# Rows of one more unit by DMA transpose, row stores moved behind two loads, and a hand-written end with stores by column halves

## The chip, the cores and the metric

The kernel runs on one core of one Trainium2 chip. The metric is the device time of one execution in microseconds (us); the time before is the median of three runs.

## The reference

Two stages follow each other, for 8 batches, 12 heads, 448 tokens and head dimension 64:

```
scores = q @ k.T / sqrt(64);  attn = max(scores, 0)**2 / 448;  o = attn @ v
x = o with the heads side by side            # (8, 448, 768)
s = x @ w_gate                               # one score per token
top = the 128 tokens of the batch with the highest score
out = x;  out[top] = x[top] + sigmoid(s[top]) * (max(x[top] @ w1, 0) @ w2)
```

`w1` is 768 x 1024, `w2` is 1024 x 768. Inputs and output are float32; the kernel computes in bfloat16 with float32 accumulation.

## The kernel before

The attention is cut into 24 units of four heads; unit u belongs to batch u // 3. Per unit the steps are: `L` loads q, k and v (a casting DMA from POOL's queue), `T` and `TE` transpose q and k on TensorE and copy them out of PSUM, `S` computes scores, `R` applies the relu on ACT or VectorE, `Q` squares, `V` multiplies with v, and `X` copies the result out as `xT_sb`, which holds x transposed: features on partitions, tokens along the row.

The rows of x (tokens on partitions, `x_rows`, tile name x_sb) are made from `xT_sb` in one of two ways. `XR` (lines 265 to 273) does eight TensorE transposes into a PSUM pair and `XE` (line 275) copies them out; `XB` (line 282) does two DMA transposes, issued from SP. Units up to 14 use the first way, units from 15 on the second. `ST` (line 291) stores the rows of a batch to the output from POOL's queue, four DMAs a batch.

The mixture-of-depths part of a batch is the class `Moe`. `g` and `bc` give the scores along the row, `col` gives them down the partitions, `rk`, `cs`, `rank` and `hot` make `hot_`, a 0/1 matrix that picks the 128 tokens by rank. `sel`, `xe` and `xeE` gather the tokens (as `xeT`), `h` and `hE` do the first layer, `gs` and `sig` the gate, `y` and `yE` the second layer times the gate (tile `gye`), and `ADD` adds the result to the stored rows by an indirect DMA from POOL.

The last batch (7) does not go through `ST` and `ADD`. There the rows are put together on TensorE: for each of four chunks c of the tokens, `xa` multiplies the rows by a permuted identity (`ident_2`) into a PSUM pair, and `od` adds the second layer's result by `hotT`, the transposed `hot_` (`ht`, `htE`). The result is split into a high and a low bfloat16 part, `yH` on ACT and `yL` on VectorE. `oE` copies a chunk out of PSUM and `OS` stores it, from SP's queue. Chunk 3 has 64 rows, the others 128. The columns come in two halves of 384, h = 0 and 1; the two halves of a tile lie in the two banks of one PSUM pair. `hq` and `yq` are `h` and `y` in parts.

The order of all instructions is written out by hand in the string `ORDER`; every item is a call, and each engine and queue takes its instructions in that order. Four PSUM pairs (0 to 3) are shared by all steps; the last number of an item that opens a tile in PSUM names its pair, and the item waits until the pair's last user is done. Waits between engines are put in from the tiles that instructions read and write. Line numbers of helpers recur in the profile: L187 is any copy on ACT, L191 a copy on VectorE, L299 any matmul of the `Moe` class, L270 the transposes of `XR`, L288 the DMA transposes of `XB`, L294 the stores of `ST`, L510 the stores of `OS`.

Of the kernel before, what the change touches and what calls it, by code (L numbers as in the profile page):

```python
# [7 lines left out]
FP32 = mybir.dt.float32  # L8
# [12 lines left out]
def kernel(  # L21
# [13 lines left out]
    B, H, S, Dh = q.shape  # L35
    HD = H * Dh
    F = moe_w1.shape[1]
    CAP = int(moe_capacity)
    NC = 7
# [16 lines left out]
    gye_pool = ctx.enter_context(tc.tile_pool(name="gye", bufs=3))  # L56
# [6 lines left out]
          for n in "qkv"}  # L63
# [3 lines left out]
    bc_sb = [const.tile([128, NK * 128], FP32, name=f"bc_sb{i}") for i in range(NX)]  # L67

    stage = {n: const.tile([128, 2, NC * Dh], FP32, name=f"{n}f") for n in "qk"}
    fin = [stage[n].rearrange("p a b -> p (a b)")[:, :HD].rearrange("p (a d) -> p a d", a=2)  # L70
           for n in "qk"]
    wgr = const.tile([NM, 128], FP32, name="wgr")
    wgb = const.tile([NM, 128], BF16, name="wgb")
    unit_f = const.tile([1, 1], FP32, name="unit_f")
# [2 lines left out]
    ident_2 = const.tile([128, 128], BF16, name="ident_2")  # L77
# [93 lines left out]
    def pair(at, shape, dt, name):  # L171
        return ps_pool.tile(shape, dt, name=name, tag=f"pair{at}")
# [12 lines left out]
    def put(eng, out_, in_, func=None, scale=1.0):  # L185
        if eng == "A":
            nc.scalar.activation(out=out_, in_=in_, func=func or AF.Copy, scale=scale)  # L187
        elif func == AF.Relu:
            nc.vector.tensor_scalar(out=out_, in0=in_, scalar1=0.0, scalar2=None, op0=ALU.max)  # L189
        elif isinstance(scale, float) and scale == 1.0:  # L190
            nc.vector.tensor_copy(out=out_, in_=in_)  # L191
        else:
            nc.vector.tensor_scalar(out=out_, in0=in_, scalar1=scale, scalar2=None, op0=ALU.mult)

    t_ps, qkt, s_ps, r_sb, o_ps, xr_ps, x_rows = {}, {}, {}, {}, {}, {}, {}
# [102 lines left out]
    def mm(out_, lhsT, rhs, start, stop, **kw):  # L298
        nc.tensor.matmul(out=out_, lhsT=lhsT, rhs=rhs, start=start, stop=stop,  # L299
                         skip_group_check=True, **kw)  # L300

    class Moe:
# [151 lines left out]

        def yq(self, half, part, at=None):
            if at is not None:
                self.y_ps = [pair(at, [CAP, 2, 512], FP32, "y_ps")] * 2
                self.y_done = [0, 0]
            for f in range(4 * part, 4 * part + 4):
                self.y(half, f)  # L460

# [20 lines left out]
                out=self.yp["L", half], in0=self.y_ps[half][:, half, :384],  # L482
                scalar=self.g_[:, 0:1], in1=self.yp["H", half], op0=ALU.mult, op1=ALU.subtract)

        def xa(self, c, at):
            self.o_ps = getattr(self, "o_ps", {})
            self.o_ps[c] = pair(at, [128, 2, 512], FP32, "od_ps")
            for h in range(2):
                mm(self.o_ps[c][:self.n_out(c), h, :384], self.side(ident_2, c),
                   x_rows[self.b][:, c, 384 * h:384 * h + 384], True, False)  # L490

        def od(self, c, l, h):
            mm(self.o_ps[c][:self.n_out(c), h, :384], self.side(self.hotT[:, c, :], c),
# [7 lines left out]
            return t if c + 4 < NC else t[:, ::2]  # L501

        def oE(self, c, h, eng):
            if c == len(fin):
                fin.append(gye_pool.tile([CAP, 2, 384], FP32, name="gye"))
            n = self.n_out(c)
            put(eng, fin[c][:n, h], self.o_ps[c][:n, h, :384])

        def OS(self, c):
            nc.sync.dma_start(  # L510
                out=out[self.b].rearrange("(p c) d -> p c d", c=NC)[:, c::4],
                in_=fin[c][:self.n_out(c)].rearrange("p a d -> p (a d)"))

        def yE(self, half, eng):
            j = slice(0, 2) if half == 2 else slice(half, half + 1)
# [62 lines left out]
    S,15,2,0 T,16,q,3 V,13,1,0,2 L,k,7,0,2 V,13,2,1 R,15,2,A V,13,3,2 S,15,0,1 V,13,4,3 Q,14,4,7,D L,q,7,0,2  # L578
    V,13,5,4 V,13,6,5 R,15,0,A V,14,1,0,0 V,13,0,6 ADD,2 V,14,2,1 V,14,3,2 X,13,A cs,3,1 TE,16,b,D V,14,4,3
    V,14,5,4 V,14,6,5 V,14,0,6 S,15,3,2 L,v,6,0,2 rank,3 hot,3 X,14,A S,15,1,3 g,4,0,0,4,1 R,15,3,D R,15,1,A  # L580
    XR,14,0 g,4,4,4,6 L,v,6,2,4 XE,14,D sel,3,3 XR,13,2 bc,4,A sE,3,0 Q,15,0,4,D S,15,4,0 XE,13,A xe,3,4 xe,3,5
    xe,3,1 xe,3,3 R,15,4,A xe,3,0 xe,3,2 ST,4,3 col,4 sE,3,1 xeE,3,2,A S,15,5,0 ST,4,1 colE,4 rk,4,0 S,15,6,2
    S,16,4,1 R,15,5,A ST,4,0 h,3,0,3 R,15,6,D h,3,3 ST,4,2 R,16,4,A h,3,7 rk,4,1 S,16,2,0 S,16,0,2 rk,4,2 R,16,2,A
    h,3,2 rk,4,3 h,3,5 Q,15,4,7,D h,3,1 R,16,0,A S,16,1,0 T,17,q,1 T,17,k,1 R,16,1,A S,16,6,2 h,3,4 TE,17,b,D
    L,q,7,2,4 R,16,6,A h,3,6 V,15,1,0,0 L,k,7,2,4 V,15,2,1 hE,3,2,A S,16,5,1 S,16,3,2 V,15,3,2 R,16,5,D V,15,4,3
    V,15,5,4 R,16,3,A V,15,6,5 V,15,0,6 T,18,q,3 Q,16,4,7,D T,18,k,3 X,15,A S,17,0,1 L,v,6,4,6 y,3,0,0,2 y,3,1,0
    y,3,0,1 y,3,1,1 R,17,0,A S,17,6,0 TE,18,b,D XB,15 y,3,0,5 y,3,1,5 R,17,6,A y,3,0,2 y,3,1,2 L,k,7,4,6 S,17,3,1
    Q,16,0,4,D S,17,1,3 R,17,3,A S,17,2,0 L,q,7,4,6 y,3,0,6 y,3,1,6 y,3,0,7 y,3,1,7 R,17,2,A gs,3,1 y,3,0,4
# [21 lines left out]
    rk,6,3 V,21,5,4 Q,22,4,7,D V,22,1,0,1 ADD,5 V,21,6,5 V,21,0,6 R,23,2,A cs,6,2 V,22,2,1 V,22,3,2 X,21,A rank,6  # L610
    S,23,0,0 hot,6 S,23,1,2 ST,6,1 V,22,4,3 V,22,5,4 R,23,0,A R,23,1,D V,22,6,5 ST,6,2 V,22,0,6 XB,21 sel,6,3
    X,22,A ST,6,0 S,23,6,0 sE,6,0 Q,23,0,4,D S,23,4,2 ST,6,3 xe,6,4 R,23,4,A xe,6,5 xe,6,3 xe,6,1 xe,6,0 R,23,6,A
    xe,6,2 g,7,0,0,4,2 sE,6,1 XB,22 xeE,6,2,A Q,23,4,7,D VO,23,0 V,23,1,0,1 V,23,2,1 V,23,3,2 h,6,0,3 h,6,1
    V,23,4,3 V,23,5,4 V,23,6,5 V,23,0,6 h,6,2 X,23,A,0 X,23,D,1 h,6,4 h,6,3 h,6,7 XB,23 h,6,6 h,6,5 colm,7,0,4
    hE,6,2,A colm,7,4,6 g,7,4,4,6 gs,6,0 rk,7,2 y,6,0,0,3 y,6,1,0 sig,6 rk,7,3 y,6,0,3 y,6,1,3 rk,7,1 y,6,0,5
    y,6,1,5 y,6,0,2 y,6,1,2 rk,7,0 y,6,0,4 y,6,1,4 y,6,0,7 y,6,1,7 cs,7,2 y,6,0,1 y,6,1,1 rank,7 hot,7 y,6,0,6
    y,6,1,6 yE,6,2,A Z,p xa,7,0,1
    ht,7,2 xeh,7,0,0 htE,7,D xeh,7,1,2 ADD,6 xeE,7,0,A hq,7,0,0,0 xeE,7,1,A hq,7,0,1 hq,7,1,0,2 hE,7,0,A hq,7,1,1
    gs,7,0 yq,7,0,0,3 hE,7,1,A sig,7 yq,7,1,0 yq,7,1,1 yq,7,0,1 xa,7,1,2 xa,7,2,0 yH,7,1 yH,7,0 yL,7,1 yL,7,0
    od,7,0,H,1 od,7,1,H,1 od,7,2,H,1 od,7,0,H,0 od,7,1,H,0 od,7,2,H,0 od,7,0,L,1 od,7,0,L,0  # L620
    oE,7,0,1,A oE,7,0,0,A od,7,1,L,1 od,7,1,L,0 oE,7,1,1,D oE,7,1,0,D OS,7,0 OS,7,1
    od,7,2,L,1 od,7,2,L,0 oE,7,2,1,A oE,7,2,0,A OS,7,2 xa,7,3,3 od,7,3,H,1 od,7,3,L,1 od,7,3,H,0 od,7,3,L,0
    oE,7,3,1,D oE,7,3,0,A OS,7,3
    """

    ms = {}
# [49 lines left out]
```

## Time and profile before

| | |
|---|---|
| median of three runs | 210.66 us (209.9, 210.66, 211.75) |
| the profiled execution | 210.09 us, of which the span of the profile is 208.3 us |
| TensorE busy | 182.9 us (88% of the span) |
| VectorE busy | 175.1 us (84%) |
| ACT busy | 170.2 us (82%) |
| POOL busy | 111.2 us (53%) |
| chain that ended last | TensorE 59%, ACT 20%, VectorE 8%, POOL 5%, DMA 3%, issue 2% |
| HBM read, written | 39.32 MB, 13.76 MB: 255 GB/s over the span |

Busy time is summed over the instructions of an engine. The chain is followed back from the last instruction of the span, at each step to what released it, so it tells which engine's work could not have been later; an engine can be busy for long and hardly stand in it. Times in rows are us from the start of the span, durations of single instructions ns or us as the column says.

### The profile page before, as it was taken

How to read it: one execution, taken by the hardware profiler on the slowest of the kernel's cores; microseconds unless marked ns; L12 is line 12 of the kernel's file. 1: busy time of each engine (PE TensorE's matmuls, PEld its weight loads, DVE VectorE, ACT ScalarE, POOL GpSimd, SP SyncE). 2: the span in 40 equal slices, each digit the busy share in tenths (PEclk: the TensorE clock that was granted, in tenths of full speed). 3: DMA queues.
4: the chain of work that ended last, by engine and by line, in shares of the span. 5: the costliest groups of instructions: out<-in, count | busy, mean ns of one | idle time of the engine just before them, and what ended most of it. 6: DMA issues, size and time to landing. Idle time of an engine off the chain costs nothing.

```text
span 208.3 us, 8440 instructions
## 1 busy us (share of the span) xinstructions
PE 182.9 (88%) x3781; PEld 119.0 (57%) x3781; DVE 175.1 (84%) x239; ACT 170.2 (82%) x219; POOL 111.2 (53%) x187
## 2 busy tenths in 40 slices
PE   1697866779999999999999999999999899997970
PEld 0443532545676666756855576567557645675730
DVE  3899998999999998998999998997989999742050
ACT  3399998999997989899989699998998989533250
POOL 7987867675677748679393945453243005303000
PEclk9999999999999999999999999999999999999996
DMA  6999999999999999999999998999397040993306
GB/s 190 166 170 201 205 201 204 207 204 202 209 315 338 215 163 168 315 131 168 174 205 260 161 283 158 145 155 134 67 283 119 6 99 5 247 223 41 61 35 229
DMA packets 35967, 36.78 MB, mean 177 GB/s; under 512 B 12566, under 2 KB 32028, under 8 KB 35932
## 3 DMA queue, kind: packets, MB, share of 16 engines
q0 software_dynamic: 25072, 31.60, 83.2%
q1 hardware_dynamic: 10860, 4.66, 12.6%
q8 instruction: 29, 0.48, 0.9%
q14 instruction: 6, 0.05, 0.1%
HBM read 39.32 MB, written 13.76 MB: 255 GB/s over the span
## 4 chain that ended last, share of the span: by engine, by line
PE 59%; ACT 20%; DVE 8%; POOL 5%; DMA 3%; issue 2%; POOLq 0%; ACTq 0%; DVEq 0%
ACT r_sb L187 15%; PE y_ps L299 11%; PE o_ps L250 11%; PE s_ps L228 10%; PE h_ps L299 10%; PE sc_ps L299 4%; PE xe_ps L299 4%; PE t_ps L209 4%; DVE r_sb L240 4%; DMA k_sb<-in_k_dram 3%; ACT xT_sb L187 3%; DVE r_sb L189 2%; PE xr_ps L270 2%; ACT gye L187 2%; PE od_ps L299 1%
## 5 line engine op out<-in xcount | busy, mean ns | idle before, releaser
L187 ACT ACTIVATE r_sb<-s_ps 128x896 bf16<-128x896 f32 x142 | 122.3, 943 | 10.6 <-PE s_ps L228 10.0
L240 DVE TENSOR_TENSOR r_sb<-r_sb 128x3584 bf16<-128x3584 bf16 (+1 forms) x48 | 85.0, 1785 | 2.4 <-ACT r_sb L187 1.4
L228 PE MATMUL s_ps<-qkt 64*64 64x448 bf16 x680 | 57.4, 377 | 6.4 <-ACT r_sb L187 4.3
L250 PE MATMUL o_ps<-r_sb,v_sb 64*64 64x448 bf16 x672 | 42.7, 351 | 2.9 <-issue 1.4
L228 PEld LDWEIGHTS <-qkt 64*64 64x64 bf16 x680 | 21.8, 108 | 24.8 <-issue 17.0
L519 POOL DMA_INDIRECT out_dram<-gye,idx x7 | 13.5, 1922 | 33.7 <-DVE mask L347 15.7
L189 DVE TENSOR_SCALAR r_sb<-s_ps 128x896 bf16<-128x896 f32 x26 | 28.1, 1087 | 2.7 <-PE s_ps L228 2.6
L105 POOL DMA_DIRECT2D v_sb<-in_v_dram x48 | 28.8, 683 | 0.5 <-DMA k_sb<-in_k_dram 0.4
L250 PEld LDWEIGHTS <-v_sb 64*64 64x64 bf16 x672 | 20.3, 106 | 12.3 <-issue 5.6
L191 DVE COPY qkt<-t_ps 128x1792 bf16<-128x1792 bf16 x24 | 25.9, 1084 | 0.8 <-PE t_ps L209 0.7
L299 PE MATMUL y_ps<-w_sb,hT 128*128 128x384 bf16 x128 | 25.5, 327 | 0.0
L299 PE MATMUL h_ps<-xeT,w_sb 128*128 128x128 bf16 x384 | 24.9, 219 | 0.2 <-ACT xeT L187 0.2
L101 POOL DMA_DIRECT2D q_sb<-in_q_dram x23 | 17.4, 754 | 13.9 <-PE t_ps L209 8.5
L299 PEld LDWEIGHTS <-w_sb 128*128 128x128 bf16 x384 | 21.7, 98 | 4.9 <-issue 4.4
L187 ACT ACTIVATE xT_sb<-o_ps 128x896 bf16<-128x896 f32 (+1 forms) x22 | 20.5, 932 | 3.6 <-PE o_ps L250 2.1
L101 POOL DMA_DIRECT2D k_sb<-in_k_dram x23 | 17.1, 744 | 9.1 <-PE s_ps L228 4.4
L294 POOL DMA_DIRECT2D out_dram<-x_sb x28 | 15.6, 625 | 11.5 <-DMA x_sb<-xT_sb 5.5
L103 POOL DMA_DIRECT2D v_sb<-in_v_dram x24 | 17.0, 710 | 7.0 <-PE s_ps L228 3.2
L299 PEld LDWEIGHTS <-hT 128*128 128x128 bf16 x128 | 10.3, 97 | 9.1 <-issue 4.3
L209 PE MATMUL t_ps<-ident,q_sb 64*64 64x64 bf16 x672 | 10.6, 200 | 5.5 <-POOL slot_i L148 4.6
L209 PEld LDWEIGHTS <-q_sb 64*64 64x64 bf16 x672 | 9.5, 113 | 8.2 <-ACT q_sb L187 4.6
L209 PE MATMUL t_ps<-ident,k_sb 64*64 64x64 bf16 x672 | 10.7, 200 | 2.1 <-ACT k_sb L187 1.1
(144 smaller groups left out, 190.5 us busy)
## 6 DMA issues: line engine op xcount, KB each, us to landing
out_dram<-x_sb POOLq DMA_DIRECT2D x21, 384.0 KB, 5.4
q_sb<-in_q_dram POOLq DMA_DIRECT2D x23, 224.0 KB, 6.2
k_sb<-in_k_dram POOLq DMA_DIRECT2D x23, 224.0 KB, 5.9
v_sb<-in_v_dram POOLq DMA_DIRECT2D x24, 112.0 KB, 5.7
v_sb<-in_v_dram POOLq DMA_DIRECT2D x48, 56.0 KB, 5.3
w_sb<-in_moe_w_dram POOLq DMA_DIRECT2D x8, 192.0 KB, 6.4
w_sb<-in_moe_w_dram POOLq DMA_DIRECT2D x6, 256.0 KB, 6.7
out_dram<-x_sb POOLq DMA_DIRECT2D x7, 192.0 KB, 4.8
```

Source lines behind the costliest of these rows:

```text
L101: nc.gpsimd.dma_start(out=t, in_=s_)
L103: nc.gpsimd.dma_start(out=t[:, 0], in_=s_[:, 0])
L105: nc.gpsimd.dma_start(out=t[64 * h:64 * h + 64, 1], in_=s_[64 - 64 * h:128 - 64 * h, 1])
L187: nc.scalar.activation(out=out_, in_=in_, func=func or AF.Copy, scale=scale)
L189: nc.vector.tensor_scalar(out=out_, in0=in_, scalar1=0.0, scalar2=None, op0=ALU.max)
L191: nc.vector.tensor_copy(out=out_, in_=in_)
L209: nc.tensor.matmul(out=t_ps[u][64 * w:64 * w + 64, g, o:o + 64], lhsT=s_[rows, w, c * Dh:c * Dh + Dh], rhs=ident[rows, rows], is_transpose ...
L228: nc.tensor.matmul(out=s_ps[u, c][64 * (g ^ w):64 * (g ^ w) + 64, w, :S], lhsT=qkt[u][rows, g, S + c * 64:S + c * 64 + 64], rhs=qkt[u][row ...
L240: (nc.gpsimd if eng == "P" else nc.vector).tensor_tensor(out=a, in0=a, in1=a, op=ALU.mult)
L250: nc.tensor.matmul(out=o_[64 * g:64 * g + 64, w, :S], lhsT=sb["v"][u % NR][rows, w, c * Dh:c * Dh + Dh], rhs=r_sb[u][rows, c, w, :], start ...
L294: nc.gpsimd.dma_start(out=out[b].rearrange("(p c) d -> p c d", c=NC)[:, 4 * g + k0:4 * g + k0 + n], in_=x_rows[b][64 * g:64 * g + 64, k0:k ...
L299: nc.tensor.matmul(out=out_, lhsT=lhsT, rhs=rhs, start=start, stop=stop, skip_group_check=True, **kw)
```

## The change

Three parts of the order change, with the helpers that they call.

- `XR,14` and `XE,14` are replaced by `XB,14`, two DMA transposes from SP at the place where `XR,14` stood.
- The four `ST,4` items, which stood spread over the items after `xeE,3` and `colE,4`, now stand together behind `L,q,7,2,4 L,k,7,2,4`.
- The end of batch 7 is written anew. `Z,p`, which makes `ident_2` on ACT, moves from behind `yE,6` to before the last square. `xa` takes a column half; `yq` gives each column half its own PSUM pair; `oE` has a tile for each chunk and half; `OS` stores one column half, or both for chunk 2. Both halves of chunk 2 share a new `gye` tile; the halves of chunk 3 use two of the `bc_sb` tiles.

```diff
+    fin = {(c, h): fin[c][:, h:h + 1] for c in range(2) for h in range(2)}
+    for h in range(2):
+        fin[3, h] = bc_sb[h][:, None, :384]
...
         def yq(self, half, part, at=None):
             if at is not None:
-                self.y_ps = [pair(at, [CAP, 2, 512], FP32, "y_ps")] * 2
-                self.y_done = [0, 0]
+                self.y_ps = getattr(self, "y_ps", [None, None])
+                self.y_ps[half] = pair(at, [CAP, 2, 512], FP32, "y_ps")
+                self.y_done = getattr(self, "y_done", [0, 0])
...
-        def xa(self, c, at):
-            self.o_ps = getattr(self, "o_ps", {})
-            self.o_ps[c] = pair(at, [128, 2, 512], FP32, "od_ps")
-            for h in range(2):
-                mm(self.o_ps[c][:self.n_out(c), h, :384], self.side(ident_2, c),
-                   x_rows[self.b][:, c, 384 * h:384 * h + 384], True, False)
+        def xa(self, c, h, at=None):
+            if at is not None:
+                self.o_ps = getattr(self, "o_ps", {})
+                self.o_ps[c] = pair(at, [128, 2, 512], FP32, "od_ps")
+            mm(self.o_ps[c][:self.n_out(c), h, :384], self.side(ident_2, c),
+               x_rows[self.b][:, c, 384 * h:384 * h + 384], True, False)
...
         def oE(self, c, h, eng):
-            if c == len(fin):
-                fin.append(gye_pool.tile([CAP, 2, 384], FP32, name="gye"))
             n = self.n_out(c)
-            put(eng, fin[c][:n, h], self.o_ps[c][:n, h, :384])
-
-        def OS(self, c):
+            if (c, h) not in fin:
+                t = gye_pool.tile([CAP, 2, 384], FP32, name="gye")
+                fin.update({(c, 0): t[:, 0:1], (c, 1): t[:, 1:2], (c, 2): t})
+            put(eng, fin[c, h][:n, 0], self.o_ps[c][:n, h, :384])
+
+        def OS(self, c, h):
+            j = slice(0, 2) if h == 2 else slice(h, h + 1)
             nc.sync.dma_start(
-                out=out[self.b].rearrange("(p c) d -> p c d", c=NC)[:, c::4],
-                in_=fin[c][:self.n_out(c)].rearrange("p a d -> p (a d)"))
+                out=out[self.b].rearrange("(p c) (a d) -> p c a d", c=NC, a=2)[:, c::4, j],
+                in_=fin[c, h][:self.n_out(c)])
...
-    XR,14,0 g,4,4,4,6 L,v,6,2,4 XE,14,D sel,3,3 XR,13,2 bc,4,A ...
+    XB,14 g,4,4,4,6 L,v,6,2,4 sel,3,3 XR,13,2 bc,4,A ...
...
-    ... xeE,3,2,A S,15,5,0 ... ST,4,3 col,4 ... ST,4,1 colE,4 ... ST,4,0 h,3,0,3 ... ST,4,2 R,16,4,A ...
+    L,q,7,2,4 R,16,6,A h,3,6 V,15,1,0,0 L,k,7,2,4 V,15,2,1 ST,4,3 ST,4,1 ST,4,0 ST,4,2 hE,3,2,A ...
...
-    y,6,1,6 yE,6,2,A Z,p xa,7,0,1
-    ht,7,2 xeh,7,0,0 htE,7,D xeh,7,1,2 ADD,6 xeE,7,0,A hq,7,0,0,0 xeE,7,1,A hq,7,0,1 hq,7,1,0,2 hE,7,0,A hq,7,1,1
-    gs,7,0 yq,7,0,0,3 hE,7,1,A sig,7 yq,7,1,0 yq,7,1,1 yq,7,0,1 xa,7,1,2 xa,7,2,0 yH,7,1 yH,7,0 yL,7,1 yL,7,0
-    od,7,0,H,1 od,7,1,H,1 od,7,2,H,1 od,7,0,H,0 od,7,1,H,0 od,7,2,H,0 od,7,0,L,1 od,7,0,L,0
-    oE,7,0,1,A oE,7,0,0,A od,7,1,L,1 od,7,1,L,0 oE,7,1,1,D oE,7,1,0,D OS,7,0 OS,7,1
-    od,7,2,L,1 od,7,2,L,0 oE,7,2,1,A oE,7,2,0,A OS,7,2 xa,7,3,3 od,7,3,H,1 od,7,3,L,1 od,7,3,H,0 od,7,3,L,0
-    oE,7,3,1,D oE,7,3,0,A OS,7,3
+    y,6,1,6 yE,6,2,A xa,7,0,0,1
+    xeh,7,0,0 xeh,7,1,2 ADD,6 xeE,7,0,A ht,7,3 htE,7,D xeE,7,1,A hq,7,0,0,0 hq,7,0,1 gs,7,3 hq,7,1,0,2 hE,7,0,A sig,7
+    hq,7,1,1 yq,7,1,0,3 xa,7,0,1 hE,7,1,A yq,7,1,1 yH,7,1 xa,7,1,1,2 yL,7,1 xa,7,1,0 yq,7,0,0,0 yq,7,0,1
+    yH,7,0 od,7,0,H,1 od,7,1,H,1 yL,7,0 od,7,0,L,1 oE,7,0,1,A OS,7,0,1 od,7,1,L,1 oE,7,1,1,A OS,7,1,1
+    xa,7,2,1,3 xa,7,2,0 od,7,2,H,1 od,7,2,L,1 od,7,2,H,0 od,7,0,H,0 od,7,0,L,0 oE,7,0,0,D OS,7,0,0
+    od,7,2,L,0 oE,7,2,1,A od,7,1,H,0 od,7,1,L,0 oE,7,1,0,A OS,7,1,0 oE,7,2,0,D OS,7,2,2
+    xa,7,3,1,0 xa,7,3,0 od,7,3,H,1 od,7,3,L,1 od,7,3,H,0 od,7,3,L,0 oE,7,3,1,D oE,7,3,0,A OS,7,3,1 OS,7,3,0
```

## Rows read from the trace of the kernel before

**Rows 1.** Chain that ended last, last 20 us: start, length, what
```profile
189.56 0.22 ACT ident L187
...
200.04 2.08 PE od_ps L299 x11
```

**Rows 2.** Timeline of the end: start, length, engine, line, operation, count, idle before
```profile
188.05 0.69 DVE L368 TENSOR_TENSOR hot__4649<-slot_row,rank__4652 128x512 bf16<-128x512 bf16 x1
...
189.83 0.50 PE L299 MATMUL od_ps<-x_sb,ident 128*128 128x384 bf16 x2 [1.25 <-ACT ident L187]
...
190.38 1.77 PE L299 MATMUL xe_ps<-hot__4649,x_sb 128*128 128x128 bf16 x24
190.58 0.69 DVE L191 CAST hotT<-ht_ps 128x512 bf16<-128x512 f32 x1 [1.84 <-PE ht_ps L299]
191.25 0.49 ACT L187 ACTIVATE xeT<-xe_ps 128x384 bf16<-128x384 f32 x1 [1.48 <-PE xe_ps L299]
...
192.00 2.91 PE L299 MATMUL h_ps<-xeT,w_sb 128*128 128x128 bf16 x48
...
193.60 0.60 ACT L187 ACTIVATE hT<-h_ps 128x512 bf16<-128x512 f32 x1 [0.92 <-PE h_ps L299]
...
194.90 2.76 PE L299 MATMUL y_ps<-w_sb,hT 128*128 128x384 bf16 x16
...
197.49 0.81 PE L299 MATMUL od_ps<-x_sb,ident 128*128 128x384 bf16 x4
197.75 1.05 ACT L187 ACTIVATE yH<-y_ps,g__4655 128x384 bf16<-128x384 f32 x2 [2.15 <-PE y_ps L299]
...
198.84 1.14 DVE L481 SCALAR_TENSOR_TENSOR yL<-y_ps,g__4655,yH 128x384 bf16<-128x384 f32 x2 [7.56 <-ACT yH L187]
...
202.73 0.48 ACT L187 ACTIVATE gye<-od_ps 64x384 f32<-64x384 f32 x1 [0.69 <-DVE gye L191]
```

**Rows 3.** Timeline of SP's DMA issues, last 11 us
```profile
201.29 0.66 SPq L510 DMA_DIRECT2D out_dram<-qf  x1
202.05 0.54 SPq L510 DMA_DIRECT2D out_dram<-kf  x1
202.68 1.41 SPq L510 DMA_DIRECT2D out_dram<-gye  x2
```

**Rows 4.** DMA issues of the end: count, KB each, us from issue to landing
```profile
out_dram<-qf SPq DMA_DIRECT2D x1, 384.0 KB, 2.8
...
out_dram<-gye SPq DMA_DIRECT2D x1, 192.0 KB, 3.6
```

**Rows 5.** Windows: length, busy PE, PEld, DVE, ACT, POOL, PEclk, DMA share, GB/s
```profile
3.00:3.50 0.50, 0.00 (x0) 0.00 (x0) 0.00 (x0) 0.00 (x0) 0.50 (x1) 1.00 1.02 384
...
188.00:188.50 0.50, 0.50 (x4) 0.12 (x2) 0.47 (x2) 0.00 (x0) 0.00 (x0) 1.00 0.08 10
...
202.50:202.70 0.20, 0.00 (x0) 0.00 (x0) 0.19 (x1) 0.00 (x0) 0.00 (x0) 1.00 0.51 200
...
203.00:203.50 0.50, 0.00 (x0) 0.00 (x0) 0.00 (x0) 0.21 (x1) 0.00 (x0) 1.00 1.00 399
```

**Rows 6.** Timeline of SP: the last two DMA transposes
```profile
184.10 3.24 SPq L288 DMA_TRANSPOSE x_sb<-xT_sb  x2
```

**Rows 7.** Chain that ended last, 117 to 155 us
```profile
117.94 0.45 PE xr_ps L270 x8
...
138.05 1.45 PE xe_ps L299 x24
...
153.52 0.48 PE t_ps L209 x56
```

**Rows 8.** Timeline of VectorE and POOL, 118 to 130 us
```profile
118.43 0.69 DVE L191 COPY x_sb<-xr_ps 128x1024 bf16<-128x1024 bf16 x1 [0.39 <-PE xr_ps L270]
...
121.65 1.57 POOL L294 DMA_DIRECT2D out_dram<-x_sb  x3 [0.44 <-DMA out_dram<-gye,idx]
...
128.85 0.55 POOL L103 DMA_DIRECT2D v_sb<-in_v_dram  x1 [1.56 <-PE o_ps L250]
```

More of the change, by code (lines that the diff above doesn't have):

```diff
@@ L580 @@
     V,14,5,4 V,14,6,5 V,14,0,6 S,15,3,2 L,v,6,0,2 rank,3 hot,3 X,14,A S,15,1,3 g,4,0,0,4,1 R,15,3,D R,15,1,A
-    XR,14,0 g,4,4,4,6 L,v,6,2,4 XE,14,D sel,3,3 XR,13,2 bc,4,A sE,3,0 Q,15,0,4,D S,15,4,0 XE,13,A xe,3,4 xe,3,5
-    xe,3,1 xe,3,3 R,15,4,A xe,3,0 xe,3,2 ST,4,3 col,4 sE,3,1 xeE,3,2,A S,15,5,0 ST,4,1 colE,4 rk,4,0 S,15,6,2
-    S,16,4,1 R,15,5,A ST,4,0 h,3,0,3 R,15,6,D h,3,3 ST,4,2 R,16,4,A h,3,7 rk,4,1 S,16,2,0 S,16,0,2 rk,4,2 R,16,2,A
+    XB,14 g,4,4,4,6 L,v,6,2,4 sel,3,3 XR,13,2 bc,4,A sE,3,0 Q,15,0,4,D S,15,4,0 XE,13,A xe,3,4 xe,3,5
+    xe,3,1 xe,3,3 R,15,4,A xe,3,0 xe,3,2 col,4 sE,3,1 xeE,3,2,A S,15,5,0 colE,4 rk,4,0 S,15,6,2
+    S,16,4,1 R,15,5,A h,3,0,3 R,15,6,D h,3,3 R,16,4,A h,3,7 rk,4,1 S,16,2,0 S,16,0,2 rk,4,2 R,16,2,A
     h,3,2 rk,4,3 h,3,5 Q,15,4,7,D h,3,1 R,16,0,A S,16,1,0 T,17,q,1 T,17,k,1 R,16,1,A S,16,6,2 h,3,4 TE,17,b,D
-    L,q,7,2,4 R,16,6,A h,3,6 V,15,1,0,0 L,k,7,2,4 V,15,2,1 hE,3,2,A S,16,5,1 S,16,3,2 V,15,3,2 R,16,5,D V,15,4,3
+    L,q,7,2,4 R,16,6,A h,3,6 V,15,1,0,0 L,k,7,2,4 V,15,2,1 ST,4,3 ST,4,1 ST,4,0 ST,4,2 hE,3,2,A S,16,5,1 S,16,3,2 V,15,3,2 R,16,5,D V,15,4,3
     V,15,5,4 R,16,3,A V,15,6,5 V,15,0,6 T,18,q,3 Q,16,4,7,D T,18,k,3 X,15,A S,17,0,1 L,v,6,4,6 y,3,0,0,2 y,3,1,0
@@ L612 @@
     X,22,A ST,6,0 S,23,6,0 sE,6,0 Q,23,0,4,D S,23,4,2 ST,6,3 xe,6,4 R,23,4,A xe,6,5 xe,6,3 xe,6,1 xe,6,0 R,23,6,A
-    xe,6,2 g,7,0,0,4,2 sE,6,1 XB,22 xeE,6,2,A Q,23,4,7,D VO,23,0 V,23,1,0,1 V,23,2,1 V,23,3,2 h,6,0,3 h,6,1
+    xe,6,2 g,7,0,0,4,2 sE,6,1 XB,22 xeE,6,2,A Z,p Q,23,4,7,D VO,23,0 V,23,1,0,1 V,23,2,1 V,23,3,2 h,6,0,3 h,6,1
     V,23,4,3 V,23,5,4 V,23,6,5 V,23,0,6 h,6,2 X,23,A,0 X,23,D,1 h,6,4 h,6,3 h,6,7 XB,23 h,6,6 h,6,5 colm,7,0,4
```

## The prediction

> **What bounds the kernel now.** I read the views in this order: the table of times, the chain that ended last, the timeline of the last 20 us, the SP queue with its landings, the DMA share in short windows, and last the stretch around 118 us. Until about 185 us the chain runs almost entirely through TensorE, ACT and VectorE, handing over between them, and each of the three is about full; the reader should see there that work taken off one engine is worth at most what the next one lets through. From 188.6 us on the picture is another: one batch is left, nothing lies beside it, and every wait is paid in full. The chain goes y, an ACT copy, `ident_2` on ACT, TensorE again, `hotT` on VectorE, xe, h, y, two yH, two yL, eleven od matmuls, two copies of the last chunk [rows 1, 2]. Then SP issues four row stores within 2.6 us [rows 3], which land 2.8 to 3.6 us after their issue [rows 4] while the DMA engines run at their full share, near 0.4 MB per us [rows 5]. The third and fourth are issued in a row [rows 3]; at SP's pitch of 0.63 the last starts at 203.3 and lands 3.6 later, at 206.9 [rows 4]; the span ends at 208.3, so 1.4 follow the landing. About 1% (2.1 us) is what a measurement here can tell from no change.
>
> **The middle: the fifteenth unit's rows (XR,14 and XE,14 become XB,14).** Removed are eight transposes on TensorE, 0.45 us of the chain [rows 7], and one VectorE copy of 0.69 [rows 8]. The gate matmuls behind them still wait for the same ACT copy (X,14), so at most 0.45 comes through on TensorE. Added are two transposes on SP, whose queue holds nothing else until unit 15's. Their cost on the queue is bounded by the last pair, 3.24 us for two [rows 6]; the rows are read first by xe of batch 4 at 138.05 [rows 7], some 17 us after, so their landing hides behind the work of batch 3. If that cover went, xe would wait for the landing, a few us at most. Of the 0.45 I take 0.3, because ACT is full behind this point; bounds 0 (ACT eats it) and 0.7 (VectorE's copy counts too). A loss is excluded by the distance to the readers, below.
>
> **The fifth batch's row stores.** Four POOL issues, 2.1 us (1.57 for three of them [rows 8]), pass two loads. Those loads started when TensorE freed their buffers, not when the stores were out, so they gain nothing; the next loads, at 128.85 [rows 8], now come behind the stores, so at most 2.1 late. A store and a load also wait for a transfer eight POOL issues back: the store at 121.65 waited 0.44 for the indirect store [rows 8]. That can hold the loads behind by 2 us or so more. They fill buffers of units 20, 22 and 23, and TensorE transposes unit 22 at 153.5 [rows 7], over 20 us on. Price: nothing, from either side.
>
> **The end, step by step** (TensorE slots: 48 h matmuls and 6 small gs in 2.90, from 192.00 to 194.90, so 0.057 for one h or xe and 0.16 for gs; 16 y in 2.59 up to the hand-over at 197.49, so 0.162 for one of 384 columns [rows 2]).
> 1. TensorE sat 1.25 idle for `ident_2`, which ACT made behind the y copy [rows 1, 2]. Now it is made earlier on an idle ACT, and the first xe may start when `hot_` is there, 188.05 + 0.69 + 0.06 = 188.80, not 190.38. The DMA transposes it reads have nothing left to move after 188.05 (share 0.08) [rows 5].
> 2. The second xe half waited for `hotT` [rows 2], which held its PSUM pair; now ht comes after both. 24 xe and four ht (0.23): 188.80 + 1.37 + 0.23 = 190.40 for the start of h, was 192.00: 1.6 gained. The xeT copy of the first half (0.49 [rows 2]) is done by then.
> 3. h and gs, 2.90: y starts at 193.30.
> 4. y goes half by half, each in its own PSUM pair. Half 1: eight y, one xa and 0.05 of waiting for hT (0.60 on ACT): 194.81. yH 0.26 later (as 197.49 to 197.75) and 0.57 long: 195.64; yL 0.61: 196.3. Meanwhile TensorE does two xa and half 0: 196.43; yH to 197.26, yL to 197.91. Both were through at 200.0 [rows 1, 2].
> 5. The first od half is done at 196.92; ACT copies it (0.49, after yH) until 197.77, and SP issues its store at 197.81, was 201.29 [rows 3]. In all 20 od and xa matmuls follow 196.43: 199.67, then 0.25 and the two copies of 64 rows, ACT's 0.48 and VectorE's taken as much, still one after the other [rows 2]: the last copy ends at 200.9.
> 6. Seven stores instead of four. SP's pitch was 0.63 (202.05 to 202.68) [rows 3]: the last is issued at 197.81 + 6 x 0.63 = 201.59, later than its data, so SP's queue is what ends last. 203.3 before: 1.7 gained.
> 7. Data began to move 1.3 after the first issue [rows 3, 5], and 0.5 passed between its last data and its landing (2.8 - 1.3 - 1.0 for 384 KB). The queue no longer piles up: half a chunk, 0.197 MB, takes 0.52 at 0.38 MB per us, less than the pitch; the whole third chunk ends at 202.6, the two quarters need 0.27 each, the last from 202.9: landing at 203.7, was 206.9. So 3.2 gained.
>
> Here stands the one unknown price: a packet of half the length (1536 bytes, was 3072). Kindest bound: half the time, as with the loads of 1792 bytes at the start, which moved 384 GB/s at full share, against 399 for the stores [rows 5]. Worst bound: the same time for each; 16 engines at 399 GB/s take 0.123 for 3072 bytes, and 40 short with 8 long packets each would take 5.9 from 199.1, landing at 205.5. I take the first, whose row is nearest in length.
>
> [...]
>
> Sum: -3.2 at the end, -0.3 in the middle, -3.5. The profiled execution took 210.09, which gives 206.6; it lies 0.57 under the median of the runs, 210.66, against which I forecast **207.2**.
>
> **Rivals.**
> - *Packets cost by number, not bytes.* All landings come at 205.5, 1.4 earlier than now; with 0.3 that is 209.0, within 1%. For it: nothing but that no store of this shape was seen. Against: [rows 5]. Chance 0.13.
> - *The wait of yL stays.* yL of half 1 started only after both yH, though it needs one [rows 2]. I put that down to the shared PSUM tile, which the change splits. If it is something else, everything from step 5 on comes 0.95 later: 208.1. Still faster; 0.12, part of the forecast's side.
> - *SP becomes the brake (slower).* Seven issues stand in a row on one queue. At the pitch of SP's transposes, 3.24 for two [rows 6], the last issue comes at 197.81 + 6 x 1.62 = 207.5 and lands at 209.6: 2.7 later than now, less 0.3, so 213.1. It decides from a pitch of 1.2; 1% is lost from 1.57. For it: a store by columns has one dimension more. Against: the four stores, 0.54 to 0.7 each [rows 3]. Chance 0.07, with whatever else costs over 1%. [...]
> - *The end is late for another reason*, so that only steps 1 to 3 pay and half of it is lost at the copies: -1.5, 209.2. Chance 0.08.
>
> **Numbers.** Forecast 0.72 (0.60 as reckoned, 0.12 with the wait of yL), within 1% 0.21, slower 0.07. The range starts from 0.7 in the middle and 0.5 of a copy's end hidden, plus the profiled execution's own base: 205.6. Upwards it takes in the packet bound, 209.0, and the late end, 209.2, and stops at 209.6.
>
> **What would show it.** Right: TensorE's gap before the first od gone; xe from about 188.8 (earlier if the middle gave its 0.3), first store at 197.8 or before, seven issues 0.6 apart, DMA share below full between them, a last landing 2.1 after its issue. Wrong: DMA at full share until 205 (packets); issues over 1.2 apart (SP); yL starting behind the second yH; or a chain around 118 to 140 us that has grown, with loads or xe of batch 4 waiting for a transfer.

## The result, and the profile after

The changed kernel takes 207.93 us (median of 20 runs), the kernel before 210.14 (20 runs): a ratio of 0.9876, with a 95% interval of 0.9846 to 0.9907, or 2.6 us less. Ratios compare only the faster executions of each kernel (within 1.5% of its fastest), so the 2.6 is more than the 2.2 between the medians, and the profiled execution, 210.20 us (span 208.4), is not among them. Forecast were 3.5 less. The profile holds one loss that a second profile of the same kernel (e11 below, 208.90 us) has in a smaller size, and that loss is what this document is about. Before it, the new end.

The timeline of the end after the change (start, length, engine, line, operation, count, idle before) answers to [rows 2]. Everything in it stands 3.52 us later than it would have from the old start: the last group of y of batch 6 starts at 191.27, and started at 187.75 before (the first row is of the kernel before, all others of the kernel after).

```profile
187.75 0.82 PE L299 MATMUL y_ps<-w_sb,hT 128*128 128x384 bf16 x4
```

```profile
191.27 0.82 PE L302 MATMUL y_ps<-w_sb,hT 128*128 128x384 bf16 x4
...
191.57 0.69 DVE L371 TENSOR_TENSOR hot__4641<-slot_row,rank__4644 128x512 bf16<-128x512 bf16 x1
...
191.93 0.33 PE L302 MATMUL od_ps<-x_sb,ident 128*128 128x384 bf16 x1
...
192.32 1.51 PE L302 MATMUL xe_ps<-hot__4641,x_sb 128*128 128x128 bf16 x24
...
193.89 1.50 PE L302 MATMUL h_ps<-xeT,w_sb 128*128 128x128 bf16 x24
...
196.72 0.81 PE L302 MATMUL y_ps<-w_sb,hT 128*128 128x384 bf16 x4
...
198.50 0.58 ACT L190 ACTIVATE yH<-y_ps,g__4647 128x384 bf16<-128x384 f32 x1 [0.98 <-PE y_ps L302]
...
199.11 0.62 DVE L485 SCALAR_TENSOR_TENSOR yL<-y_ps,g__4647,yH 128x384 bf16<-128x384 f32 x1 [4.32 <-ACT yH L190]
...
204.02 0.48 ACT L190 ACTIVATE bc_sb<-od_ps 64x384 f32<-64x384 f32 x1 [1.13 <-DVE bc_sb L194]
```

TensorE no longer stops for `ident_2`, xe starts 0.06 after `hot_`, and yL starts 0.03 after its own yH, not after both. The seven stores on SP's queue answer to [rows 3]:

```profile
201.06 0.68 SPq L517 DMA_DIRECT2D out_dram<-qf  x1
201.83 0.55 SPq L517 DMA_DIRECT2D out_dram<-kf  x1
202.50 0.54 SPq L517 DMA_DIRECT2D out_dram<-qf  x1
203.14 0.57 SPq L517 DMA_DIRECT2D out_dram<-kf  x1
203.80 0.56 SPq L517 DMA_DIRECT2D out_dram<-gye  x1
204.44 1.21 SPq L517 DMA_DIRECT2D out_dram<-bc_sb  x2
```

Their landings (count, KB each, median us from issue) answer to [rows 4]:

```profile
out_dram<-qf SPq DMA_DIRECT2D x2, 192.0 KB, 2.3
out_dram<-kf SPq DMA_DIRECT2D x2, 192.0 KB, 2.2
out_dram<-gye SPq DMA_DIRECT2D x1, 384.0 KB, 2.7
out_dram<-bc_sb SPq DMA_DIRECT2D x2, 96.0 KB, 2.3
```

And the windows (length, busy PE, PEld, DVE, ACT, POOL, PEclk, DMA share, GB/s), which answer to [rows 5]:

```profile
203.00:204.00 1.00, 0.39 (x3) 0.02 (x1) 0.64 (x2) 0.00 (x0) 0.00 (x0) 1.00 0.84 301
204.00:205.00 1.00, 0.00 (x0) 0.00 (x0) 0.00 (x0) 0.48 (x1) 0.00 (x0) 1.00 0.81 289
205.00:206.00 1.00, 0.00 (x0) 0.00 (x0) 0.00 (x0) 0.00 (x0) 0.00 (x0) 1.00 1.01 389
```

(A share above 1.00, as the 1.01 here, means that packets overlap: their times are added up.) The stores leave the DMA engines room (shares of 0.84 and 0.81) until the whole chunk comes, and each lands 2.2 to 2.7 after its issue, where the last took 3.6. From y to the end of the span the old kernel took 208.3 - 187.75 = 20.55 us, the new one 208.4 - 191.27 = 17.13: 3.4 less.

So, by these two profiles, the end won more than the whole, and the middle gave back. Here is VectorE's copy of the transposed q and k (a mark that every unit has), first of the kernel before, then after; the change's first edit lies between the first two marks.

```profile
115.00 1.08 DVE L191 COPY qkt<-t_ps 128x1792 bf16<-128x1792 bf16 x1
...
125.84 1.09 DVE L191 COPY qkt<-t_ps 128x1792 bf16<-128x1792 bf16 x1
...
140.87 1.09 DVE L191 COPY qkt<-t_ps 128x1792 bf16<-128x1792 bf16 x1 [0.39 <-PE t_ps L209]
...
150.04 1.08 DVE L191 COPY qkt<-t_ps 128x1792 bf16<-128x1792 bf16 x1
```

```profile
115.54 1.08 DVE L194 COPY qkt<-t_ps 128x1792 bf16<-128x1792 bf16 x1
...
125.71 1.09 DVE L194 COPY qkt<-t_ps 128x1792 bf16<-128x1792 bf16 x1
...
142.66 1.09 DVE L194 COPY qkt<-t_ps 128x1792 bf16<-128x1792 bf16 x1 [2.24 <-PE t_ps L212]
...
153.46 1.08 DVE L194 COPY qkt<-t_ps 128x1792 bf16<-128x1792 bf16 x1
```

Between the first two marks the kernel before takes 10.84 us, the changed one 10.17: 0.67 less. From the second to the third, at 140.87 and 142.66, they take 15.03 and 16.95: 1.92 lost, and 1.6 more are lost by the next of these copies, at 153.46 (150.04 before). (The first mark is 0.54 late ahead of any edit.) Where they went is seen on TensorE at 140, in the kernel after:

```profile
140.00 0.20 PE L212 MATMUL t_ps<-ident,k_sb 64*64 64x64 bf16 x4
142.22 0.38 PE L212 MATMUL t_ps<-ident,k_sb 64*64 64x64 bf16 x24 [2.02 <-issue]
```

Four of the 28 transposes of unit 21's k are done, then nothing for 2.02 us, then the other 24. All 28 read the same tile and write the same tile, so no data can have been missing between the fourth and the fifth. "Issue" means that TensorE waited for nothing that the profile shows. The same windows as above, after the gap:

```profile
142.00:143.00 1.00, 0.78 (x36) 0.57 (x40) 0.34 (x1) 0.00 (x0) 0.00 (x0) 0.96 1.13 191
143.00:144.00 1.00, 1.00 (x16) 0.56 (x12) 0.76 (x1) 0.65 (x1) 0.00 (x0) 0.50 1.46 148
144.00:146.00 2.00, 2.00 (x26) 0.94 (x19) 0.78 (x1) 1.40 (x3) 0.90 (x2) 0.50 1.37 102
```

Behind the 2.02 us in which TensorE stood idle the granted clock fell to 0.50, in the windows from 143 to 146; of the 3.52 us that this execution is late at the end, 2.0 are the gap, and the 1.6 behind it were lost between 142.66 and 153.46, the stretch with these windows.

**The theory (A).** What TensorE lacked were its own instructions, and they come over the DMA engines too. The page's list of DMA queues has a queue of instructions (packets, MB, share of 16 engines), with packets of 16 KB:

```profile
q8 instruction: 29, 0.48, 0.9%
```

Whose instructions these are the page does not say. It counts 3773 matmuls and 3773 weight loads on TensorE, about 260 to a packet; that the packets bring TensorE's stream, and that TensorE stops when the next one (a refill) is late, is assumed here and tested below. The theory goes on: when the four stores (1.4 MB) and two more transposes stand on the DMA engines ahead of a refill, it comes late. That there is a backlog is seen in the windows and in the landings of the transposes issued between 130 and 134 us, first of the kernel before, then after:

```profile
138.00:139.00 1.00, 1.00 (x22) 1.00 (x19) 1.00 (x3) 1.00 (x2) 1.00 (x3) 1.00 1.03 194
x_sb<-xT_sb SPq DMA_TRANSPOSE x2, 6.4
```

```profile
138.00:139.00 1.00, 1.00 (x19) 1.00 (x19) 1.00 (x3) 1.00 (x2) 1.00 (x3) 1.00 1.92 113
x_sb<-xT_sb SPq DMA_TRANSPOSE x2, 9.2
```

**Rival B:** the gap is chance, found in every version alike. **Rival C:** it is the loads of q, k and v, pushed back on POOL's queue, that come late.

### The profile page after: what moved, and what is told of

Its sections match the earlier page's. It is cut to its first block, busy times and chain, and to the rows that moved or that the text cites. A ratio compares the mean times of both kernels' runs of the same rounds, so it can differ in the third digit from the quotient of the medians.

```text
span 208.4 us, 8434 instructions
## 1 busy us (share of the span) xinstructions
PE 183.5 (88%) x3773; PEld 119.5 (57%) x3773; DVE 175.1 (84%) x238; ACT 170.3 (82%) x219; POOL 111.1 (53%) x187
## 4 chain that ended last, share of the span: by engine, by line
PE 61%; DMA 12%; ACT 9%; DVE 6%; POOL 6%; issue 3%; POOLq 0%; DVEq 0%
PE s_ps L231 11%; PE y_ps L302 10%; PE h_ps L302 10%; PE o_ps L253 10%; ACT r_sb L190 7%; DMA w_sb<-in_moe_w_dram 6%; DMA k_sb<-in_k_dram 6%; PE xe_ps L302 5%; PE t_ps L212 5%; PE sc_ps L302 4%; DVE r_sb L243 3%; DVE r_sb L192 2%; PE od_ps L302 2%; POOL q_sb L104 2%; POOL v_sb L108 2%
## 5 line engine op out<-in xcount | busy, mean ns | idle before, releaser
L302 PE MATMUL y_ps<-w_sb,hT 128*128 128x384 bf16 x128 | 25.9, 328 | 0.0
L302 PE MATMUL h_ps<-xeT,w_sb 128*128 128x128 bf16 x384 | 25.4, 221 | 0.2 <-ACT xeT L190 0.2
L212 PE MATMUL t_ps<-ident,q_sb 64*64 64x64 bf16 x672 | 11.1, 200 | 5.4 <-POOL chunk_no L150 4.5
```

Of the source, the lines that this page charges most:

```text
L212: nc.tensor.matmul(out=t_ps[u][64 * w:64 * w + 64, g, o:o + 64], lhsT=s_[rows, w, c * Dh:c * Dh + Dh], rhs=ident[rows, rows], is_transpose ...
```

## The experiments

Three groups of four, each on one chip beside the kernel before. Each ratio is to the kernel before of its group. "Gap" is TensorE's idle time at the one place of its stream, in the one profiled execution.

| kernel | median us (runs) | ratio, 95% interval | gap us |
|---|---|---|---|
| e1 the end alone | 207.05 (6) | 0.9848 (0.9792 to 0.9903) | none |
| e6 the middle alone | 211.94 (12) | 1.0067 (1.0025 to 1.0108) | 1.39 |
| e4 end and XB,14 | 208.92 (12) | 0.9904 (0.9857 to 0.9950) | 0.95 |
| e5 end and moved stores | 209.84 (12) | 0.9983 (0.9941 to 1.0024) | 0.55 |
| e7 end and two idle loads | 209.37 (12) | 0.9958 (0.9919 to 0.9997) | 1.34 |
| e8 change, stores later | 206.86 (6) | 0.9849 (0.9793 to 0.9906) | none |
| e9 end, four whole stores | 207.77 (6) | 0.9882 (0.9842 to 0.9922) | 0.20 |
| e10 end, stores later | 207.81 (12) | 0.9877 (0.9843 to 0.9910) | none |
| e11 the change again | 208.38 (6) | 0.9895 (0.9838 to 0.9952) | 1.39 |
| e12 e1 again | 207.31 (6) | 0.9836 (0.9784 to 0.9888) | none |
| e13 e8 again | 206.90 (6) | 0.9844 (0.9793 to 0.9895) | none |
| e14 change, no row stores | 206.21 (6) | 0.9802 (0.9757 to 0.9847) | 0.69 |

**e1, the end alone.** The changed kernel with the middle put back; the four ST,4 stand again where the kernel before has them.

```diff
-    XB,14 g,4,4,4,6 L,v,6,2,4 sel,3,3 ...
+    XR,14,0 g,4,4,4,6 L,v,6,2,4 XE,14,D sel,3,3 ...
-    L,k,7,2,4 V,15,2,1 ST,4,3 ST,4,1 ST,4,0 ST,4,2 hE,3,2,A ...
+    L,k,7,2,4 V,15,2,1 hE,3,2,A ...
```

> Only the new end; XR,14, XE,14 and the four ST,4 as before. Theory A (the end is worth its whole 3.4 us, counted from y of batch 6 in the two profiles, and the middle part gives 0.6 in the chain but makes TensorE run out of instructions in some executions): 3.0 to 3.5 us below the kernel before, so a ratio of 0.984 to 0.986, no gap of 2 us on TensorE between 135 and 145 us, and a mean clock near 1. Rival B (the end is worth only the 2.6 us that the whole change measured, the middle nothing, and the gap is chance that every version has): 2.6 us below, and times as scattered as the whole change's.

3.2 us below (210.56 x 0.0152), no gap. That is near the 3.4 of the two profiles; the interval, 2.0 to 4.4 us, does not by itself leave out the 2.6 of rival B. Its six runs lie within 1.4 us, but that was luck: as e12 it went from 205.58 to 210.32, with the same median to 0.3.

**e6, the middle alone.** The same two edits made in the kernel before.

> Only the middle: XB,14 and the moved ST,4 as in the change, the end as before. Theory A: about 0.6 us below the kernel before where TensorE does not run dry, 1 to 3 us above where it does, so scattered over more than 3 us and near 0 to +1.5 in the median. Rival B: within 0.5 us of the kernel before and no wider scatter.

0.7% slower, an interval that leaves out no change. The middle costs, in itself, with the old end behind it. The scatter decides nothing: 4.5 us here, and 4.5 in the kernel before beside it. The gap is there:

```profile
142.74 0.38 PE L209 MATMUL t_ps<-ident,k_sb 64*64 64x64 bf16 x24 [1.39 <-issue]
```

**e4 and e5, one half of the middle each.** e4 puts the stores back, e5 the TensorE transposes.

> The new end and XB,14, but the four ST,4 at their old places, where they may have to wait for the transposes on POOL's queue. If the moved stores are what holds up TensorE's instructions (A1): tight, 3.5 to 4 us below the kernel before. If the added transposes are (A2): scattered as the whole change. Rival B: 2.6 below.

> The new end and the moved ST,4, but XR,14 and XE,14 on TensorE and VectorE as before. A1 (stores hold up the instructions): scattered as the whole change, with gaps on TensorE in some executions. A2 (the transposes do): tight, 3.0 to 3.5 us below the kernel before. Rival B: 2.6 below.

Both lie above the end alone, e5 with its interval clear of e1's, e4's overlapping it. Neither A1 nor A2 holds alone: each half brings a gap, and each median is above e1's (for e4 that is likely, not shown). Rows of e4, of e5, and of the kernel before at that place:

```profile
140.68 0.38 PE L212 MATMUL t_ps<-ident,k_sb 64*64 64x64 bf16 x24 [0.95 <-issue]
```

```profile
140.97 0.38 PE L253 MATMUL o_ps<-r_sb,v_sb 64*64 64x448 bf16 x4 [0.55 <-DMA q_sb<-in_q_dram]
```

```profile
140.20 0.38 PE L250 MATMUL o_ps<-r_sb,v_sb 64*64 64x448 bf16 x4 [0.17 <-issue]
```

Read the place, not only the length. Where there is a gap, it stands ahead of the fifth transpose of k in every kernel with XB,14 (the change, e4, e6, and below e11 and e14), and ahead of V in every kernel without it (before, e5, e7, e9). Between the two lie four V and four transposes, each a weight load and a matmul: 16 instructions, and XR,14 was eight transposes, 16 instructions. Taking 16 instructions out of the stream moves the gap 16 instructions on. A gap between two blocks of the stream does that; for a wait for data there is no reason to. (In e5 the profile names a load of q as what ended the wait; V reads v and r, no q.)

The count can be taken further. Number TensorE's instructions (matmuls and weight loads) in the traces by their start: in all nine profiles with a gap it ends at the same number, 5569. Some of the kernels stop elsewhere too, and those places are whole blocks of 256 away: at 5313 in e11, at 4033 in e6 (1.06 us, ahead of any edit), at 5825 in e7. Rows of these three:

```profile
134.71 0.21 PE L212 MATMUL t_ps<-ident,q_sb 64*64 64x64 bf16 x1 [0.54 <-issue]
```

```profile
104.79 0.28 PE L209 MATMUL t_ps<-ident,q_sb 64*64 64x64 bf16 x10 [1.06 <-issue]
```

```profile
148.91 1.31 PE L305 MATMUL sc_ps<-xT_sb,wg_rep 128*128 128x448 bf16 x6 [1.13 <-ACT r_sb L193]
```

So rival B has a part of the truth: a stop at some boundary is found in most versions. What the middle changes is its size at this one. The kernels that keep the old middle (before, e1, e12, e9) have 0.17, none, none and 0.20 there, those with the new one (the change, e11, e6) 2.02, 1.39 and 1.39.

**e7, two loads that nobody reads.** The end alone, plus:

```diff
+        elif what == "d":
+            for n in "qk":
+                nc.sync.dma_start(out=stage[n], in_=head_src(n, 0, 0, 2))
...
-    ... xe,4,5 XB,16 T,21,q,3 ...
+    ... xe,4,5 Z,d XB,16 T,21,q,3 ...
```

> The end-only kernel plus two loads of 448 KB from SP, issued behind XB,15 (about 132 us), into two tiles that nothing reads then. Theory A (TensorE's own instructions come by DMA, one packet of 16 KB at a time, and a backlog of data on the DMA engines between 130 and 140 us makes TensorE run dry at one fixed place of its stream, just ahead of V of unit 17 before the k transposes of unit 21): a gap of 1 to 3 us on TensorE at that place with no tile to wait for, an instruction packet that comes or lasts 1 us or more longer than in the end-only kernel, and 1 to 3 us more time than its 207.05. Rival C (the loss of the middle comes from loads of q, k and v that arrive late): no gap at that place but TensorE waiting on a q, k or v transfer. Rival B (chance): as the end-only kernel, within 0.5 us.

2.3 us above e1 in the median, and the intervals of the two ratios are (just) apart. Nothing reads these tiles, yet TensorE stops at the place, and once more one block on (the row at 148.91 above); the two stops make 2.46 of the 2.6 us by which this profile's span is longer than e1's:

```profile
141.88 0.38 PE L256 MATMUL o_ps<-r_sb,v_sb 64*64 64x448 bf16 x4 [1.34 <-issue]
```

The instruction packet ahead of it is found in the window 139.0 to 139.5; in e1 in 137.5 to 138.0, and in the change, whose gap is longest, in 138.5 to 139.0, but there it took twice as long. The rows of e7, e1 and the change (packets, MB, share of 16 engines in a window of 0.5 us: 14.2% is 1.1 us of one engine, 12.0% is 1.0, 25.9% is 2.1):

```profile
q8 instruction: 1, 0.02, 14.2%
```

```profile
q8 instruction: 1, 0.02, 12.0%
```

```profile
q8 instruction: 1, 0.02, 25.9%
```

How long the packet takes does not decide: in e14 below it takes 3.0 us, with a gap of 0.69, in e4 1.0, with a gap of 0.95. When it ends does. From the moment when TensorE passes the boundary before (number 5313) to the end of the packet it is 4.0 to 4.6 us in the five kernels without a gap, and then 5.1 (before), 5.3 (e9), 5.8 (e5), 5.8 (e14), 6.2 (e4), 6.4 (e7), 6.5 (e6), 6.5 (e11) and 7.3 (the change): the order of the gaps. And TensorE goes on 1.30 to 1.39 us after the end of the packet in all nine with a gap; in the five without one it comes to the place 1.48 us behind the packet or later. These times are read from the packets' own records in the traces. Over whole traces the 29 packets come one for each 256 TensorE instructions, and in the 392 crossings of the 14 profiles TensorE is never less than 1.1 us behind its packet. So at these stops TensorE waits for its instructions: by these times that step is shown, not argued.

**e8, the stores moved on.** The change, with its stores past the crowded stretch. **e10** is the same without XB,14.

```diff
-    L,k,7,2,4 V,15,2,1 ST,4,3 ST,4,1 ST,4,0 ST,4,2 hE,3,2,A ...
+    L,k,7,2,4 V,15,2,1 hE,3,2,A ...
-    X,17,A R,18,0,D h,4,0,2 L,v,7,2,4 h,4,7 ...
+    X,17,A R,18,0,D h,4,0,2 L,v,7,2,4 ST,4,3 ST,4,1 ST,4,0 ST,4,2 h,4,7 ...
```

> The whole change with the four ST,4 moved on once more, behind L,v,7,2,4 (issued near 143 us), so that their 1.4 MB is out of the stretch before TensorE's refill. Theory A: the gap shrinks from 1 to 2 us to some 0.5 or less, and the time falls below the whole change's 207.93, to 206 to 207, with less scatter. Rival C or B: as the whole change, 207.5 to 208.5.

> The end-only kernel (XR,14 and XE,14 on TensorE and VectorE) with the four ST,4 behind L,v,7,2,4. Theory A: no gap of TensorE at its refill, as tight as the end-only kernel, within 0.5 us of its 207.05. If moving the stores costs in itself, wherever they go: near the 209.84 of the kernel with the end and the moved stores.

e8 came as expected: no gap, 206.86. e10 has no gap in its profile either, but its runs go from 205.62 to 210.73 and its median is 0.8 above e1's: not as tight as expected. Where the longer ones lose is not known: the profile is of the shortest.

**e9, whole stores.** The end alone, with four stores instead of seven; the copies keep their order, and those of chunk 3 go into one `gye` tile (that edit is left out here).

```diff
-    ... oE,7,0,1,A OS,7,0,1 od,7,1,L,1 oE,7,1,1,A OS,7,1,1
+    ... oE,7,0,1,A od,7,1,L,1 oE,7,1,1,A
-    ... oE,7,0,0,D OS,7,0,0 ... oE,7,1,0,A OS,7,1,0 ... OS,7,3,1 OS,7,3,0
+    ... oE,7,0,0,D OS,7,0,2 ... oE,7,1,0,A OS,7,1,2 ... OS,7,3,2
```

> The end-only kernel with four whole stores instead of seven: chunk 0, 1, 2 and 3, each when both halves are copied. By the working of the prediction SP issues the last store when the last copy is done (about 201.0 in its count instead of 201.6) but the stores start 1.2 us later and pile up: four stores of 1.38 MB from 200.3 at 0.39 MB per us land at about 204.3, 0.6 later than by halves; so 0.4 to 0.8 us above the end-only kernel. If packets cost by number (the rival of the prediction): 0.5 us or more below it.

0.7 above e1 in the median (by the ratios, 0.0034 or 0.7 us as well), within what was expected; the intervals overlap. So e9 alone does not show a difference. The mechanism shows in the landings: whole stores pile up as they did in [rows 4], 2.8 for the first and 3.6 for the last, where the seven take 2.2 to 2.7. And it shows in the packets: at the end of the changed kernel one of 1536 bytes takes 66 ns in the median, one of 3072 bytes 124. Here packets did not cost by number.

**e11 to e14, one chip.** e11 is the change, e12 is e1, e13 is e8; e14 is the change without its four stores.

> The whole change, beside its variants on one chip. Theory A: 0.5 to 1.5 us above the end-only kernel and the one with later stores, with a gap on TensorE at its refill near 140 us. Rival B: level with both.

> The end-only kernel again, as the base for the other three: 3.0 to 3.5 us below the kernel before, no gap of over 0.5 us at the refill. If its first six times were luck, its median comes near the whole change's.

> The whole change with the stores behind L,v,7,2,4, again beside the others. Theory A: 0.5 to 1 us below the whole change and level with the end-only kernel or up to 0.6 below it. Rival B: level with the whole change.

> The whole change without the four ST,4: batch 4's rows are not stored, 1.4 MB less on the DMA engines after 127 us, nothing else changed on any engine. Theory A: TensorE finds its instructions in time or nearly so (gap under 0.5 us), 1 to 2 us below the whole change. If the two added transposes alone hold the refill up, whatever the stores do: the gap stays near 1 us and the time near the whole change's.

The order of the medians is A's: 208.38, 207.31, 206.90, 206.21; only those of e14 and the change (e11) have intervals that all but part, so the order of the others is likely, not shown. The gap of the change came back at the same instruction, and in e14, with 1.4 MB less, half of it was left, a little more than the 0.5 expected, while the time fell by 2.2, a little more too; 1.4 MB less can save time elsewhere as well. Rows of e11 and e14:

```profile
142.55 0.38 PE L212 MATMUL t_ps<-ident,k_sb 64*64 64x64 bf16 x24 [1.39 <-issue]
```

```profile
140.66 0.38 PE L212 MATMUL t_ps<-ident,k_sb 64*64 64x64 bf16 x24 [0.69 <-issue]
```

## Why the prediction was right or wrong

**The end, steps 1 to 7: right, to 0.3 us at each step.** Taking 3.52 off the rows of after: xe 188.80 (said 188.80), h 190.37 (190.40), y 193.20 (193.30), yH 194.98 (195.07), first store 197.54 (197.81), last issue about 201.5 (201.59), its landing 203.8 (203.7). Forecast was 3.2; the two profiles give 3.4, and e1 and e12, which have the end alone, 3.2 and 3.4 in the runs. That nothing lies beside it may be why it could be reckoned so closely.

**The wait of yL: right.** It went with the shared tile (199.08 to 199.11); that rival is out.

**The packets: right.** A packet of half the length took about half the time, 66 ns against 124. At this end seven stores (e1) were 0.7 us better in the median than four (e9; the intervals overlap), and the landings fit: the seven, at 2.2 to 2.7 us, do not wait behind each other, where e9's four took 2.8, 3.0, 3.5 and 3.6.

**XR,14 on TensorE: right in itself.** Between the first two marks the seven profiles with XB,14 take 10.17 to 10.20 us, the seven without it 10.28 to 11.37, with a median of 10.43. That is 0.1 at least and 0.3 by the median; the forecast took 0.3. The 0.67 of the two profiles above would be too much: the kernel before also has a stop of 0.25 at a block boundary in this stretch (at 116.14).

**The fifth batch's row stores, "Price: nothing, from either side": wrong**, and with it the sign of the middle and the sentence "A loss is excluded by the distance to the readers". The step went down the list of who waits for the transfers that are late (loads of q, k and v, xe of batch 4) and found each with some 17 us or more to spare, which held: rival C is not seen, for outside e5's stop at the boundary TensorE waits for no load longer than 0.3 us between 110 and 190 us in any of the 14 profiles. It left out one reader of the DMA engines that has no line in the kernel, TensorE's instruction stream. The words "from either side" shut the bound that would have held it. The middle was put at -0.3; measured alone it is +1.4 (e6). Beside the end it comes to +0.6 and +1.2 by the ratios (the change against e1, and e11 against e12), with intervals that overlap. The sign that was named for it, a chain around 118 to 140 us that has grown, came, but not with loads or xe waiting.

The whole came out within the range since the end's 3.2 outweighed the middle. The forecast of 3.5 less was 0.9 too much, and that is the middle's. That the range held it was luck: its upper room was made for the packets and a late end, and neither came. (Its lower end is 205.7 by its own terms, 210.09 - 3.2 - 0.7 - 0.5, not 205.6.)

**What stays open.** e5, with the moved stores and without XB,14, lost more (0.9983) than the change with both (0.9876), though its one profile, of its fastest run, has a gap of only 0.55; it has two more stops at block boundaries, 0.45 ahead of the edits and 0.30 behind. How refill, stores and transposes met on the DMA engines in the other executions, one profile a kernel does not show, and which of them holds the packet back was not separated. Nor does it show how much the clock costs in the median: behind the change's gap it fell to 0.50, and in e11 it stayed at 1.00 from 140 to 150 us behind a gap of 1.39, in e7 at 1.00 from 140 to 148 behind one of 1.34.

**A better version.** e8 and e13 (the change with its stores behind L,v,7,2,4) gave 206.86 and 206.90, ratios 0.9849 and 0.9844, against 0.9876 and 0.9895 for the change; the intervals overlap, so this is likely, not shown. The end alone is level with it.

## What to carry to other kernels

When a transfer moves, ask not only which tile is late, but what else is queued on the DMA engines there: in this fully unrolled kernel TensorE's instructions came the same way, in 29 packets of 16 KB. A gap of 2.02 us marked "issue" in the middle of a run of equal matmuls was its sign here (though the profile named a load in e5, and ACT at e7's second stop). The tests are to count: here such stops were whole multiples of 256 TensorE instructions apart, and at the one boundary they ended 1.30 to 1.39 us behind a packet of the instruction queue. And to move it: a few instructions more or less ahead of it, or a transfer that nobody reads. Row by row reckoning was good to 0.3 us where one batch is left with nothing beside it, and missed the sign where the engines are all full.

## What the runs showed of the hardware

- TensorE ran dry between two packets of its instruction stream for 0 to 2.02 us at one boundary, the same instruction in all nine profiles with a gap there, and in some at boundaries whole blocks of 256 instructions away (1.06 us in e6, 1.13 in e7). It went on 1.30 to 1.39 us after the end of the packet.
- The gap followed the end of the packet and not its length: 4.0 to 4.6 us after the boundary before, no gap; 7.3 us after it, 2.02. A packet of 3.0 us stood before a gap of 0.69 (e14), one of 1.0 before 0.95 (e4).
- The granted clock fell to 0.50 (143 to 146 us) behind the gap of 2.02 us. Behind the gap of 1.39 in e11 it stayed at 1.00 (140 to 150 us), and in e6, with a gap of 1.39, its mean over the span was 0.997.
- A packet of 1536 bytes took 66 ns in the median and one of 3072 bytes 124. A store of half the columns landed in 2.2 to 2.3 us; the first whole one took 2.8 in the kernel before.
